# Seven products over 1024 tokens, in six accumulator banks, with every engine in written order

## The chip, the cores and the metric

The kernel runs on one NeuronCore of one Trainium2 chip. The metric is the device time of one execution in microseconds (us). Smaller is better. A core has a matrix engine (PE, TensorE), a vector engine (DVE), an activation engine (ACT), a general engine (POOL, GpSimd), and queues from which DMA transfers are issued; SP, the sync engine, issues nearly all of them here.

## The reference

`x` is 2048 tokens of 576 numbers, all in fp32. Everything starts from the layer norm `xn` of `x`.

- Branch A is a sliding-window attention: `xn @ wqkv`, 32 heads of 18 numbers, each query sees itself and the 255 keys before it, then `@ wo`. Its result is `s`.
- Branch B is a gated unit that mixes along the tokens:

```python
z  = gelu(xn @ w_in)                 # 2048 x 4608
z1 = z[:, :2304]
z2 = layernorm(z[:, 2304:])          # over the 2304 columns
g  = w_sp @ z2 + b_sp[:, None]       # 2048 x 2048 times 2048 x 2304
B  = (z1 * g) @ w_out                # 2048 x 576
out = x + s * silu(B)
```

The product `w_sp @ z2` is the largest piece of arithmetic in the kernel. "The spatial stage" below is this product, the bias, and the multiplication with `gelu(z1)`.

## The kernel before

**fp32 on the matrix engine.** A number is split into a high part that the engine can hold and the rest: `split(hi, lo, src)` (L105 to L107) copies `src` to `hi` on ACT, and subtracts `hi` from `src` into `lo` on DVE. A product of two split operands takes three passes: high by high, high by low, low by high. So each operand of a matmul costs one ACT and one DVE instruction first, and the DVE one waits for the ACT one.

**The stages, in order of time.** (1) Layer norm of `x`, transposition, split, and the products for q and k. (2) The values, then the second half of `w_in` with its gelu (`z2`, stored to `z2_d` in DRAM, L588 to L605), while POOL forms four sums and differences of the quarters of `w_sp` (`sp_combos`, `S1` to `S4`, stored to `sc_d`). (3) Attention in 16 units of four heads and half of the tokens each; the first half of `w_in` (`z1`, before its gelu, stored to `z1_d`) is threaded into it as filler. For each unit the row maxima of the next one are found early (`row_max`), and `RM0`, `RM1`, `RMN` say over which share of the unit they are spread. (4) The output projection of the attention, `wo_tile`, with the first forming of z blocks beside it. (5) The spatial stage. (6) The last stage: `y` from DRAM, split, times `w_out`, silu, and the end result.

**Seven products.** The spatial matrix and z2 are each cut in two by two blocks over the tokens, and the block product is done with seven block products instead of eight (the Strassen-Winograd form). Its left operands are `A11`, `A12`, `A22` of `w_sp` and the four stored combinations. Its right operands are seven z blocks, `zt[0]` to `zt[6]`: three normalized blocks of z2, and four sums or differences. `z_part` forms them block by block: `norm` loads 128 x 384 of z2 and normalizes it on DVE (`tensor_scalar`, L136); POOL forms the sums (L153 to L163).

**The loop of the spatial stage.** Columns of z2 are taken in `NG` = 3 groups of 384 column pairs. For each group there are two passes `c` over the output tokens, each 512 tokens of an output block. In each pass the seven products of `ORDER` run one after the other. `product` (L779 to L797) takes four steps `q`. A step loads 128 x 1024 of the left operand (`spr`), splits it into `sph` and `spl`, splits two z blocks at once (128 x 768 into `zh`, `zl`), and issues 18 matmuls of 512 columns into three accumulators (L794). Accumulators have two sides of three banks each, `acc00` to `acc02` and `acc10` to `acc12`. A finished product is evicted by `finish`, one product later, at `q` = 0 of the next: copies on ACT, sums on DVE and POOL, the gelu of `z1` on ACT (L814), the product with it on POOL (L815), and a store to `y_d`, which is issued one product later again. `work(3)` advances the forming of the z blocks of the next group (or the loading and splitting of `w_out` in the last group) by three small pieces per step.

**What sets the order.** From stage 2 to the end of stage 4 the PE, POOL and DVE instructions run in the order in which the program writes them (`manual_schedule`). In the spatial stage before the change no engine has a written order: a planner with a model of the times orders every engine's instructions. An engine works strictly in its order; an instruction that waits holds up what stands behind it on that engine. SP is such a queue for the DMAs.

Of the kernel before, what the change touches and what calls it, by code (L numbers as in the profile page):

```python
# [16 lines left out]
P = 128  # L17
S = 2048
D = 576
# [18 lines left out]
ZRB = 5  # L38
WCB = 3
RM0 = 0.0  # L40
RM1 = 0.78
# [14 lines left out]
def kernel(  # L56
# [22 lines left out]
    sc_d = dram.tile([4, 2, 4, P, 1024], F32, name="sc_d")  # L79
# [42 lines left out]
    def z_tile(from_pool, k):  # L122
        t = from_pool.tile([P, 2 * S if k < 4 else 8 * ZW], F32, name=f"b{k}")
        return t[:, :8 * ZW].rearrange("p (s c) -> p s c", s=8)

    def z_part(from_pool, g, k):


        def norm(i, j, s, dst=None):
            raw = from_pool.tile([P, ZW], F32, name="zr", bufs=ZRB)  # L130
            t = 8 * i + s
            c0 = j * FB + g * ZW
            sp.dma_start(raw, z2_d[t * P:(t + 1) * P, c0:c0 + ZW])
            yield
            dst = raw if dst is None else dst
            dve.tensor_scalar(dst, raw, mv2[:, t, 0:1], rstd2[:, t:t + 1], ALU.subtract, ALU.mult)  # L136
            yield dst

        def run(*gens):
            for n in gens:  # L140
                next(n)
            yield
            yield [next(n) for n in gens]

        for s in range(8):
            z = zt[k][:, s]
            if k in (0, 2, 6):
                yield from run(norm(int(k > 0), int(k == 6), s, z))
            elif k == 1:
                r = run(norm(1, 1, s), norm(0, 1, s))  # L150
                yield next(r)
                b22, b12 = next(r)
                pool.tensor_tensor(b22, b22, b12, ALU.subtract)  # L153
                pool.tensor_tensor(z, b22, zt[0][:, s], ALU.add)
                yield
            elif k == 4:
                r = run(norm(0, 1, s))
                yield next(r)
                b12, = next(r)
                pool.tensor_tensor(z, b12, zt[0][:, s], ALU.subtract)  # L160
                yield
            else:
                pool.tensor_tensor(z, *((zt[1][:, s], zt[0][:, s]) if k == 3 else (zt[2][:, s], zt[1][:, s])),  # L163
                                   ALU.subtract)
                yield

    xb = [xp.tile([P, 2 * S], F32R, name=f"b{k}").rearrange("p (a s) -> p a s", a=2) for k in range(4)]
    xt = xp.tile([P, S], F32R, name="tail")
    with ExitStack() as early:
        mmp = open_pool(early, "mmp", bufs=2, space=PSUM)  # L170
        zw = open_pool(early, "zw", bufs=2)
        def passes(wh, wl, xs):
            for k in range(4):
                yield wh[:, k], xb[k][:, 0, xs]
                yield wh[:, k], xb[k][:, 1, xs]
                yield wl[:, k], xb[k][:, 0, xs]
            yield wh[:, 4], xt[:, xs]
            yield wl[:, 4], xt[:, xs]
# [6 lines left out]
        with ExitStack() as ph:  # L185
# [23 lines left out]
            def norm_chunk(c):  # L209
# [19 lines left out]
                for k in range(5):  # L229
                    t = tp.tile([P, 512], F32, name="tpt")  # L230
                    for i in range(4):
                        pe.transpose(t[:, i * P:(i + 1) * P], xs[4 * c + i][:, k * P:(k + 1) * P], ident)
                    if k < 4:
                        split(xb[k][:, 0, cs], xb[k][:, 1, cs], t)
                    else:
                        act.activation(xt[:, cs], t, AF.Copy)
                        dve.tensor_tensor(xt[64:128, cs], t[64:128], f32(xt[64:128, cs]), ALU.subtract)
# [39 lines left out]
        with ExitStack() as ph:  # L277
# [234 lines left out]
            def sp_combos(stack):  # L512

                wc = open_pool(stack, "wc", bufs=WCB)
                steps = [(c, q, slice(h * 512, h * 512 + 512)) for c in range(2) for q in range(4) for h in range(2)]

                def load(c, q, cs):
                    ts = []
                    for n, (i, j) in (("a11", (0, 0)), ("a12", (0, 1)), ("a21", (1, 0)), ("a22", (1, 1))):
                        t = wc.tile([P, 512], F32, name=n)  # L520
                        sp.dma_start(t, w_sp[2 * i + c, 4 * j + q, :, cs])
# [4 lines left out]
                for n, (c, q, cs) in enumerate(steps):  # L526
# [10 lines left out]
                    for k, t in enumerate((a22, a11, a21, a12)):  # L537
                        sp.dma_start(sc_d[k, c, q, :, cs], t)
# [3 lines left out]
            with ExitStack() as gate:  # L542
# [26 lines left out]
                for pc in range(6):  # L569
# [13 lines left out]
                    for s in range(NS):  # L583
# [11 lines left out]
                        if s % 2 == 0:  # L595
                            zt = gz.tile([P, 2 * ZW], F32, name="zt")
                        zv = zt[:, s % 2 * ZW:s % 2 * ZW + ZW]
                        act.activation(zv, ps[:, :ZW], AF.Gelu_apprx_tanh)  # L598
                        dve.bn_stats(st2[:, s, pc, :], zv)  # L599
                        if s % 2 == 1:  # L600
                            act.dma_start(z2_d[(s - 1) * P:(s + 1) * P, zc].rearrange("(a p) c -> p a c", p=P),
                                          zt[:, :2 * ZW].rearrange("p (a c) -> p a c", a=2))
# [12 lines left out]
            raws = []  # L615
# [20 lines left out]
            with ExitStack() as heads:  # L636
# [7 lines left out]
                for u in range(NU):  # L644
# [11 lines left out]
                    for t, (s, j) in enumerate(items):  # L656
# [26 lines left out]
                        if u == NU - 1 and t == 30:  # L683
                            raws += [wo_load(0)]
# [10 lines left out]

        with ExitStack() as ph:
# [3 lines left out]
            def wo_tile(t):  # L700
                orw = raws[t]
# [5 lines left out]
                for c in range(2):  # L707
# [13 lines left out]
                    act.dma_start(s_d[rows, :], so)  # L721

            bb = xp.tile([P, S], F32, name="tail")
            zt = [z_tile(xp, k) for k in range(4)]

            def first_group():
                for k in range(4):
                    yield from z_part(zp, 0, k)

            head = first_group()  # L730
            raws += [wo_load(t) for t in range(1, 4)]
            for t in range(NS // 2):
# [3 lines left out]
                for _ in range(4):  # L736
                    next(head, None)
                if 1 <= t <= 4:
                    raws += [wo_load(t + 3)]
            for _ in head:  # L740
                pass
# [266 lines left out]
```

## Time and profile before

| | us |
|---|---|
| median of 3 runs (2181.55 to 2192.11) | 2190.79 |
| the profiled execution, whole | 2182.15 |
| its span, first to last instruction | 2180.4 |
| spatial stage, first to last of its 3024 matmuls | 1138.3 to 1932.4 |
| attention projection (stage 4), its matmuls | 1059.1 to 1128.6 |
| last stage, its matmuls | 1942.2 to 2175.3 |

The page of the profile gives busy times per engine, then groups of instructions by line with busy time, mean duration and the idle time just before them. Durations of matmuls overlap, because they are pipelined: the distance between two starts is what counts. A row of a window table gives the busy time (and the number of instructions) of PE, the weight load of PE, DVE, ACT and POOL, then the granted clock of PE as a share of full speed, the share of the DMA engines and GB/s. A row of the list of waits reads: who waited, for whom, us in total, how often, the longest.

### The profile page before, as it was taken

What the parts mean: (1) busy time and instruction counts of PE and PEld (TensorE: products, weight loads), DVE (VectorE), ACT (ScalarE), POOL (GpSimd) and SP (SyncE); (2) the same over time, 40 slices, a digit from 0 to 9 for tenths busy, and PEclk for the clock granted to TensorE, in tenths of its full rate; (3) what the DMA queues carried; (4) which work ended last, traced back from release to release, by engine and by line L of the source; (5) the groups of instructions that cost most, each with busy time, mean ns of one, the idle gap of its engine ahead of it and who ended that gap; (6) DMA issues with size and microseconds to landing.
All of it is one profiled execution on the core that took longest, in us unless ns stands there. A gap on an engine that the chain in (4) does not pass through costs nothing. (4 is left out here: it accounts for less than half of the span.)

```text
span 2180.4 us, 30948 instructions
## 1 busy us (share of the span) xinstructions
PE 2018.9 (93%) x11096; PEld 1661.3 (76%) x11096; DVE 1185.5 (54%) x2140; ACT 884.2 (41%) x1547; POOL 709.7 (33%) x624
## 2 busy tenths in 40 slices
PE   6999989989999999998879988899988999979999
PEld 5889989976666666665778766677676877769999
DVE  6411322465545555653277678766788667753331
ACT  3212212235545555555334453454434555532220
POOL 4001662012222222222083447734477343310000
PEclk9999999999999999999889999999999999999999
DMA  8655895234444545453585565655656555655441
GB/s 255 163 143 178 311 376 212 80 100 124 124 132 128 142 128 146 129 128 102 186 267 191 173 222 176 217 170 168 219 177 201 173 176 184 198 193 169 153 130 45
DMA packets 218986, 375.60 MB, mean 172 GB/s; under 512 B 43216, under 2 KB 115792, under 8 KB 218704
## 3 DMA queue, kind: packets, MB, share of 16 engines
q1 hardware_dynamic: 188688, 325.79, 49.3%
q10 hardware_dynamic: 30144, 47.83, 6.1%
q8 instruction: 87, 1.43, 0.3%
q14 instruction: 67, 0.55, 0.1%
HBM read 260.45 MB, written 112.83 MB: 171 GB/s over the span
## 5 line engine op out<-in xcount | busy, mean ns | idle before, releaser
L794 PE MATMUL acc<-spl,zh 128*128 128x512 f32 x1008 | 410.6, 407 | 48.4 <-DVE spl L107 48.1
L794 PE MATMUL acc<-sph,zl 128*128 128x512 f32 x1008 | 403.1, 400 | 0.0
L340 DVE CUSTOM_DVE_ANT_0 junk<-sp,band 128x384 bf16<-128x384 f32 (+1 forms) x512 | 267.6, 537 | 224.0 <-PE sp L336 219.4
L794 PE MATMUL acc<-sph,zh 128*128 128x512 f32 x1008 | 345.3, 397 | 25.4 <-ACT sph L106 25.4
L455 ACT ACTIVATE pt<-tps 128x384 f32<-128x384 f32 (+2 forms) x576 | 248.6, 438 | 230.7 <-PE tps L451 213.2
L107 DVE TENSOR_TENSOR zl<-b,zh 128x768 fp32r<-128x768 f32 x168 | 216.3, 1288 | 153.4 <-ACT zh L106 147.2
L794 PEld LDWEIGHTS acc<-spl,zh 128*128 128x128 f32 x1008 | 195.0, 193 | 117.1 <-DVE spl L107 77.1
L107 DVE TENSOR_TENSOR spl<-spr,sph 128x1024 fp32r<-128x1024 f32 x168 | 272.1, 1620 | 16.8 <-ACT sph L106 11.7
L106 ACT ACTIVATE zh<-b 128x768 fp32r<-128x768 f32 x168 | 141.4, 842 | 263.3 <-PE acc L794 251.7
L794 PEld LDWEIGHTS acc<-sph,zh 128*128 128x128 f32 x1008 | 192.0, 192 | 71.1 <-ACT sph L106 30.8
L384 PE MATMUL mm<-b,z1wh 128*128 128x512 f32 x576 | 231.6, 413 | 0.0
L794 PEld LDWEIGHTS acc<-sph,zl 128*128 128x128 f32 x1008 | 195.2, 194 | 39.6
L451 PE MATMUL tps<-att 128*128 128x384 f32 (+1 forms) x576 | 191.8, 333 | 32.7 <-ACT pt L455 19.5
L934 PE MATMUL po<-b,yh 128*128 128x288 f32 x1152 | 202.0, 298 | 9.4 <-ACT yh L106 9.4
L458 POOL TENSOR_SCALAR_AFFINE_SELECT pt<-pt 128x512 f32<-128x512 f32 x128 | 85.6, 669 | 380.3 <-ACT pt L455 370.7
L934 PEld LDWEIGHTS po<-b,yh 128*128 128x128 f32 x1152 | 171.2, 191 | 9.9 <-ACT yh L106 9.9
L336 PE MATMUL sp<-att 128*128 128x384 f32 (+1 forms) x512 | 176.5, 346 | 2.0 <-DVE mx L340 1.6
L106 ACT ACTIVATE sph<-spr 128x1024 fp32r<-128x1024 f32 x168 | 175.4, 1045 | 0.0
L588 PE MATMUL mm<-z2wh,b 128*128 128x384 f32 x640 | 166.1, 336 | 8.6 <-ACT zt L598 8.5
L451 PEld LDWEIGHTS tps<-att 128*128 128x128 f32 x576 | 110.0, 191 | 66.3 <-ACT pt L455 35.8
L599 DVE BATCH_NORM_STATS2 st<-zt 128x6 f32<-128x384 f32 x96 | 52.8, 558 | 180.2 <-ACT zt L598 180.2
L815 POOL TENSOR_TENSOR z1t<-z1t,cb 128x512 f32<-128x512 f32 x54 | 95.2, 1788 | 149.3 <-DVE cb L823 144.2
(154 smaller groups left out, 3214.8 us busy)
## 6 DMA issues: line engine op xcount, KB each, us to landing
spr<-sc_d SPq DMA_DIRECT2D x96, 512.0 KB
spr<-in_w_sp_dram SPq DMA_DIRECT2D x72, 512.0 KB
zr<-z_d SPq DMA_DIRECT2D x144, 192.0 KB
st_d<-qkhl SPq DMA_DIRECT2D x72, 256.0 KB
z_d<-zt ACTq DMA_DIRECT2D x48, 384.0 KB
z_d<-z1o ACTq DMA_DIRECT2D x72, 256.0 KB
z1t<-z_d SPq DMA_DIRECT2D x72, 256.0 KB
y_d<-z1t SPq DMA_DIRECT2D x72, 256.0 KB
```

The lines of the kernel that those rows point to most:

```text
L106: act.activation(hi, src, AF.Copy)
L107: dve.tensor_tensor(lo, src, f32(hi), ALU.subtract)
L336: pe.matmul(ps[:, :w], q_of(u, j)[:, i * P:(i + 1) * P], k_of(u, j)[:, k0:k0 + w], start=True, stop=True)
L340: dve.tensor_tensor_reduce(out=junk[:, :w], in0=ps[:, :w], in1=band[:, m0:m0 + w], scale=1.0, scalar=-3.0e38, op0=ALU.add, op1=ALU.max, ac ...
L384: pe.matmul(ps, w, r, start=n == 0, stop=n == len(pl) - 1)
L451: pe.matmul(ps[:, :m * P], k_of(u, j)[:, (kb - base) * P:(kb - base + 1) * P], q_of(u, j)[:, (a - lo) * P:(a - lo + m) * P], start=True, s ...
L455: act.activation(pt[:, j, d0:d0 + n * P], ps[:, (qa - a) * P:(qa - a + n) * P], AF.Exp, scale=scale)
L458: pool.affine_select(out=pt[:, :, 0:P], in_=pt[:, :, 0:P], pattern=[[0, 4], [1, P]], compare_op=ALU.is_ge, fill=0.0, base=0, channel_multi ...
L588: pe.matmul(ps[:, :ZW], r, wt, start=n == 0, stop=n == len(pl) - 1)
L794: pe.matmul(acc[p], z[:, s, ps], w[:, s], start=b and n == 0, stop=e and n == 2, skip_group_check=True)
L815: pool.tensor_tensor(zs[p], zs[p], blocks[p], ALU.mult)
L934: pe.matmul(po[i][:, a, :288], y[:, i * P:(i + 1) * P], w[:, a * 288:(a + 1) * 288], start=f == 0 and m == 0, stop=f == NF - 1 and m == 2)
```

## The change

- **Shape of a product.** The two passes `c` are merged: a product now covers 1024 output tokens. It has eight steps `s`, each with one z block of 128 x 384 and one 128 x 1024 tile of the left operand, and again 18 matmuls of 512 columns, now three into each of six accumulators. The six rotate through all eight banks. There are 168 steps as before; a z block is now split once per group, not twice. The layout of `w_sp` in DRAM, `sc_d` and the loop of `sp_combos` follow.
- **Order of the products.** `A11` times z block 0, then `A12` times 2 added on top, then `S2`·1, `S3`·3 on top, `S1`·4, `S4`·6 on top, and `A22`·5. An accumulator opens anew at products 0, 2, 4 and 6 (`OPENS`).
- **No POOL work in the stage.** Normalizing goes from DVE to ACT (`Identity` with the reciprocal deviation as scale and `nmr2` as bias); sums of z blocks, sums of accumulators and the products with gelu go from POOL to DVE.
- **Written order.** All five engines run the spatial stage in program order. In the iteration of step m the program writes: the matmuls of step m; if it ends a product, its eviction; the load of the left operand for step m+4; both splits for step m+2; one or two z units (`pump`: the forming of a unit is written two units behind its loads); four deferred pieces (`run_lazy`: loads and gelus of `z1`, bias sums, products, stores).
- **The start.** The load and the splits of step 0 are written into stage 4, in a pool of their own (`w0p`), and five z blocks are formed there (four before). `b_sp` is loaded at the beginning of stage 4.
- **The end.** In the last group 14 of the 18 tiles of `w_out` are loaded and split beside the products; the other four in the last stage, one after the other through one buffer. `y` is split into eight buffers of three row tiles; its chunks are taken in the order 0 to 7.
- **Elsewhere.** `xb` and `xt` become six tiles of equal size with the same contents (`plane`), the weights of `z1` and `z2` go to the other side of the on-chip memory, the z2 result has four buffers (two before), `WCB` goes from 3 to 2, `RM1` from 0.78 to 0.70, the buffers of `zr` from 5 to 6.

The core of the diff, with the new loop:

```diff
-ORDER = [(A11, "a"), (S2, "b"), (A12, "a"), (S3, "b"), (S1, "c"), (A22, "d"), (S4, "c")]
+PRODUCTS = [(A11, 0), (A12, 2), (S2, 1), (S3, 3), (S1, 4), (S4, 6), (A22, 5)]
...
+    def split_step(m):
+        if m < len(order_sp):
+            g, n, s = order_sp[m]
+            h = [w_tile(m, [P, w], F32R, t) for t, w in
+                 (("sph", 1024), ("spl", 1024), ("zh", ZW), ("zl", ZW))]
+            split(h[2], h[3], zt[PRODUCTS[n][1]][:, s])
+            split(h[0], h[1], raws.pop(m))
+            halves[m] = h
...
+        ph.enter_context(tc.manual_schedule(engines={
+            mybir.EngineType.PE, mybir.EngineType.Activation, mybir.EngineType.DVE, mybir.EngineType.Pool,
+            mybir.EngineType.SP}))
...
+        def evict(g, n):
+            if n == 0:
+                st["t1"] = tiles("t1")
+                for j in range(6):
+                    act.activation(st["t1"][j], acc[j], AF.Copy)
+                st["z"] = z1_load(g, 0, 0)
+            elif n == 1:
+                gate(g, 0, 0, st["z"], plus(acc, lambda j: bias(j, 0)))
+            elif n == 2:
+                st["u2"] = tiles("u2")
+                for j in range(6):
+                    dve.tensor_tensor(st["u2"][j], acc[j], st["t1"][j], ALU.add)
+                    lazy.append(lambda j=j, u=st["u2"]: dve.tensor_tensor(u[j], u[j], bias(j, 0), ALU.add))
...
+        for m, (g, n, s) in enumerate(order_sp):
+            k = PRODUCTS[n][1]
+            if s == 0 and n in OPENS:
+                acc = [accp.tile([P, 512], F32, name=f"acc{(base + j) % 8}") for j in range(6)]
+                base += 6
+            wh, wl, zh, zl = halves.pop(m)
+            for j in range(6):
+                c, p = divmod(j, 3)
+                cs, ps = slice(c * 512, c * 512 + 512), slice(p * P, p * P + P)
+                for i, (z, w) in enumerate(((zh, wh), (zh, wl), (zl, wh))):
+                    pe.matmul(acc[j], z[:, ps], w[:, cs], start=s == i == 0 and n in OPENS,
+                              stop=s == 7 and i == 2, skip_group_check=True)
+            if s == 7:
+                evict(g, n)
+            load_w(m + 4)
+            split_step(m + 2)
+            pump(2 if len(units) > 4 else 1)
+            run_lazy(4)
```

`w_tile(m, ...)` takes its buffer from `w0p` for every third step and from a pool of two for the others, so three steps can be held. `gate` puts six products and six stores into the deferred list, `z1_load` six loads and six gelus.

392 lines of the change are left out of this document (182 added, 210 removed).

## The prediction

> **What bounds the kernel now.** I read the page first, then a table of windows cut at the stages, then who made PE wait.
>
> ```profile
> PE 2018.9 (93%) x11096; PEld 1661.3 (76%) x11096; DVE 1185.5 (54%) x2140; ACT 884.2 (41%) x1547; POOL 709.7 (33%) x624
> ```
>
> ```profile
> core 0: us, PE busy (x) PEld busy (x) DVE busy (x) ACT busy (x) POOL busy (x), PEclk, DMA share, GB/s
> 247.20:458.00 210.80, 202.25 (x1154) 198.77 (x1153) 78.10 (x172) 44.93 (x92) 74.66 (x56) 1.00 0.60 217
> ...
> 1138.30:1932.40 794.10, 729.99 (x3023) 576.21 (x3024) 592.81 (x532) 376.59 (x476) 380.74 (x227) 0.97 0.59 189
> 1460.00:1500.00 40.00, 39.77 (x175) 32.26 (x174) 28.70 (x26) 20.40 (x26) 14.71 (x9) 1.00 0.53 169
> 1932.40:1942.20 9.80, 0.40 (x2) 0.00 (x0) 1.20 (x2) 0.84 (x1) 3.69 (x3) 0.75 0.63 192
> 1942.20:2175.30 233.10, 233.00 (x1728) 232.76 (x1728) 67.41 (x108) 49.29 (x79) 0.00 (x0) 0.99 0.44 137
> ```
>
> PE is the bound, and the question is how far each stage is from PE's own pace. In the spatial stage a good stretch (1460 to 1500) issues 175 matmuls in 40.00 us, 0.2286 us each. At that pace its 3024 matmuls take 691 us; they take 794.1. So **103 us** of the stage are not matmul work, and no change that keeps 3024 matmuls of this form can gain more there. The last stage runs without gaps.
>
> ```profile
> PE acc L794 <- DVE spl L107: 48.1, 50, 3.8
> PE acc L794 <- ACT sph L106: 25.4, 12, 9.8
> ```
>
> PE waits for the splits: 73.5 us, of which 9.8 lie before the first matmul of the stage. Of the 103, then, some 64 are these waits; the granted clock of 0.97 costs 0.03 x 794 = 24; the rest, 15, is small gaps. The clock is a consequence of the waits:
>
> ```profile
> 1574.51 0.50 PE L794 MATMUL acc<-spl,zh 128*128 128x512 f32 x1 [2.46 <-DVE spl L107]
> ...
> 1575.65 0.63 PE L794 MATMUL acc<-spl,zh 128*128 128x512 f32 x1
> 1576.08 0.63 PE L794 MATMUL acc<-sph,zl 128*128 128x512 f32 x1
> ...
> 1578.64 0.49 PE L794 MATMUL acc<-sph,zl 128*128 128x512 f32 x1
> ```
>
> After a wait of 2.46 us, matmuls start 0.43 us apart instead of 0.23, from 1575.65 to 1578.64: seven of them, and with the two at the edges some 1.6 us lost. [...] So waits of two to four us are priced with 1.6 us on top.
>
> Why is the split late?
>
> ```profile
> 1914.60 1.23 DVE L107 TENSOR_TENSOR spl<-spr,sph 128x1024 fp32r<-128x1024 f32 x1 [0.63 <-DMA wr<-in_w_out_dram]
> ...
> 1918.54 2.31 DVE L107 TENSOR_TENSOR spl<-spr,sph 128x1024 fp32r<-128x1024 f32 x1
> 1920.77 2.05 DVE L107 TENSOR_TENSOR zl<-b,zh 128x768 fp32r<-128x768 f32 x1
> 1922.74 1.21 DVE L107 TENSOR_TENSOR spl<-spr,sph 128x1024 fp32r<-128x1024 f32 x1
> ```
>
> ```profile
> 1916.51 5.50 POOL L815 TENSOR_TENSOR z1t<-z1t,cb 128x512 f32<-128x512 f32 x3 [10.21 <-DVE cb L823]
> ```
>
> The same subtraction takes 1.23 us alone and 2.31 while POOL multiplies. POOL is busy for 381 of the 794 us, so up to half of the splits can be of the slow kind, and they queue behind loads in an order that a planner chose.
>
> **The change, part by part.** The prices come from these groups:
>
> ```profile
> L107 DVE TENSOR_TENSOR yl<-yr,yh 128x768 fp32r<-128x768 f32 x48 | 44.5, 956 | 68.6 <-ACT yh L106 68.5
> L949 DVE TENSOR_TENSOR fx<-fx,fs 128x288 f32<-128x288 f32 x32 | 13.1, 452 | 0.0
> L823 DVE TENSOR_TENSOR cb<-acc,t 128x512 f32<-128x512 f32 x36 | 22.7, 681 | 2.7 <-PE acc L794 2.7
> L106 ACT ACTIVATE sph<-spr 128x1024 fp32r<-128x1024 f32 x168 | 175.4, 1045 | 0.0
> L106 ACT ACTIVATE zh<-b 128x768 fp32r<-128x768 f32 x168 | 141.4, 842 | 263.3 <-PE acc L794 251.7
> L814 ACT ACTIVATE z1t<-z1t 128x512 f32<-128x512 f32 x72 | 45.3, 630 | 129.1 <-DMA z1t<-z_d 106.0 <-issue 22.6
> L110 ACT ACTIVATE sd<-mv,eps_t 128x4 f32<-128x4 f32 x3 | 0.9, 297 | 5.6 <-DVE mv L222 5.6
> ```
>
> *DVE.* A subtraction of 384 columns: between 452 (288 wide) and 956 (768 wide, no POOL work in that stage), by a line 553 ns. A step needs 1.22 + 0.55 = 1.77 us. Per group of 56 steps: 56 x 1.77 = 99.3; z sums 16 + 8 + 8 + 8 = 40 x 0.553 = 22.1; accumulator sums, bias sums and products 36 + 12 + 24 = 72 x 0.681 = 49.0. Together 170 us. PE needs 56 x 18 x 0.2286 = 230 us. So DVE is 74% full although it takes over POOL's work, because the splits fall back to their undisturbed length and the z split halves. *ACT.* A copy of 384: on the line through 842 and 1045, 0.54 us. Normalizing on ACT is in no row; it lies between that 0.54 and, with two operands per partition, 0.78 (297 ns for four columns against about 236 on the line puts one such operand at 0.06, and I allow twice that for each). I take 0.66. Per group 56 x 1.585 + 48 x 0.66 + 6 x 0.6 + 24 x 0.63 = 139 us, 60%. Neither is the bound on average. *DMA*: the same bytes (189 GB/s x 794 us) in 700 us, 214 GB/s, below the 217 that stage 2 had.
>
> *Cover.* The splits of step m+2 can start when step m-1 has freed its buffers and must be done at the end of m+1: two steps, 2 x 4.11 = 8.23 us, for 1.77 of DVE. This lead is what hides everything, so I walk its worst place, the end of the third product, where DVE evicts and also forms block 1. After PE's last matmul: last eviction done at 0.8; splits 1.77; two z units of two sums 2.21; four bias sums 2.72; the next splits 1.77. Sum 9.27 against 8.23: **1.0 us late**. With z blocks of one sum (ends of products 3, 4, 6, counted from 0) the sum is 8.17, just on time; elsewhere shorter. The banks cost nothing: bank j is complete three matmuls x (6 - j) before the end of a product and is wanted again in the same order. So 3 x 1.0, and I add 4 for the ends without margin. Stage: 691 + 7 + 5 (below, first steps and hand-overs) = **703, so -91 us**. Ends: -103, and -36 (the first rival).
>
> *The start of the stage.*
>
> ```profile
> 1081.22 47.34 PE L716 MATMUL wops<-att,ohl 128*128 128x288 f32 x332 [4.34 <-DVE ohl L705]
> 1138.32 1.65 PE L794 MATMUL acc<-sph,zh 128*128 128x512 f32 x3 [9.76 <-ACT sph L106]
> ```
>
> PE stands 9.8 us. After the change step 0 is split in stage 4, and PE waits only for the last eviction there, about 1.5. Step 1's operand lies in memory that stage 4 frees; load, ACT and first matmul take some 6 us against 1.5 + 4.1, so 1 to 2 us more. **-8**, between 0 and -9.
>
> *Stage 4 itself* now forms five z blocks instead of part of four, and `b_sp` (1 MB, 5 us at 217 GB/s) is loaded ahead of the rows that `wo_tile` wants. DVE has 32 sums x 0.55 = 18 us there without POOL's disturbance. **+2**, -5 to +8.
>
> *Stage 2.*
>
> ```profile
> PE mm L588 <- ACT zt L598: 8.7, 9, 2.9
> ACT zt L598 <- DMA z_d<-zt: 21.0, 6, 4.3
> ```
>
> Four buffers take away the wait of ACT for stores; PE can gain at most its 8.7. `WCB` = 2 makes SP wait for each store of a combination before the next load, 16 times, ahead of weights that have a step of slack. **-5**, -9 to +8.
>
> *`RM1`*: the maxima end earlier in a unit, so their way through DRAM ends earlier; PE's waits for it:
>
> ```profile
> PE tps L451 <- DMA att<-m_d: 13.0, 6, 6.2
> ```
>
> The 6.2 is the first unit's, which `RM1` does not touch; 6.8 is the most to gain, and denser maxima load DVE more. **-1**, -6 to +6.
>
> *The end of the stage.*
>
> ```profile
> 1932.38 3.71 POOL L815 TENSOR_TENSOR z1t<-z1t,cb 128x512 f32<-128x512 f32 x3 [10.37 <-DVE cb L823]
> ...
> 1936.49 1.54 SPq L911 DMA_DIRECT2D yr<-y_d  x3
> ...
> 1941.34 0.84 ACT L106 ACTIVATE yh<-yr 128x768 fp32r<-128x768 f32 x1 [13.75 <-issue]
> ```
>
> PE stands 9.8 us: POOL's three products, stores, then 4.85 for the load of `y`. After: last eviction 0.8, six products on DVE 4.1, perhaps a split of `w_out`, stores, the same load, 0.85: about 12. **+2**, -2 to +6. In the last stage four tiles of `w_out` come one by one, a load of up to 4.85 and a split of 1.4 each, from some 14 us after the last product: ready at 20, 26, 32 and 38. PE takes 12 x 233.1 / 1728 = 1.62 us per row tile in the first chunk, so it wants the first of them at 12 + 14 x 1.62 = 35, the last at 40. **+1**, 0 to +8. `plane`, sides of the memory and chunk order: nothing, the same instructions on the same data.
>
> Sum: -91 - 8 + 2 - 5 - 1 + 2 + 1 = **-100 us**, from the profiled execution's 2182.15 to 2082. The median of the runs stands 8.6 above the profiled execution, with one run of three at its level; I add 3: **2085 us**.
>
> **Rivals.**
>
> *DVE is the next bound (chance 0.15).* For it: 74% on average and no margin at four ends of products per group. If DVE's work took 30% longer (waits between its instructions, ACT and DVE handing over halves), the third product's end is late by 1.0 + 0.3 x 9.27 = 3.8, the three marginal ones by 2.4 each, two others by 1 or 2: 14 per group, 42 in all, plus 12 slow starts x 1.6 = 19. Stage 752, total about 2134. Against it: undisturbed DVE durations scatter by hundredths (1.21, 1.23), and the stage without POOL work runs them at 956.
>
> *The written order holds the loads up (0.06), slower than before.* SP has one queue: a store of a product waits at its head for DVE, and the load for step m+4 stands behind it. A load is written 4 steps = 16.5 us before PE wants it; minus 4.85 landing and 2.3 splitting, 9.3 us of slack. If SP is held about 13 us at each of the 21 ends, PE stands 3.7 and loses 1.6 to the clock: 21 x 5.3 = 111 on top of 703, total 2196, slower. It decides from a hold of 12.3 us (a loss of 100 / 21 = 4.8). Against it: the store is written six pieces, one and a half steps, behind its product. [...]
>
> *The change does not do what it says (0.06).* Of the waits only the part that POOL's disturbance made goes, and ACT, now ordered, stands behind gelus that wait for `z1` (106 us of ACT's waits are for that load): half of the 91 stays, 2130 to 2150; or all of it, within 0.5% (0.02).
>
> *Better (0.07)*: the walk's lateness does not show, stage 2 gains its 8.7 and the start its 9: 2050 to 2062.
>
> **How the numbers follow.** Forecast (2062 to 2110): 0.64. About 0.5% is what can be told from no change here. Faster: 0.64 + 0.15 + 0.06 + 0.07 = 0.92; same 0.02; slower 0.06. The range reaches down into the better case and up to the end of the DVE rival, 2055 to 2136; outside are the upper part of "does not do", "same", "slower" and a little below.
>
> **What would show it.** POOL at 0 in the stage; `spl` at 1.22 and a z split near 0.55 in every instance; 3024 matmuls in about 700 us at a clock of 0.99 or more; PE's waits for `spl` and `sph` under 10 us, the longest in the second and third step after the third product; one wait near 2 us at the start. DVE near 510 us busy in the stage, ACT near 420. Wrong if PE still waits tens of us for splits, if SP's rows show issues held for over 10 us, or if the stages before 1056 move by more than 10 us.

## The result and the profile after

The changed kernel takes **2075.29 us** (median of 4 runs, 2071.18 to 2077.59); the kernel before took 2188.66 in the same comparison (four runs, 2181.55 to 2192.11; the table above has three of them). The ratio is **0.9484**, 95% interval 0.9454 to 0.9514: faster. The forecast was 2085 us, with a range of 2055 to 2136.

Windows of the changed kernel, cut at the same events as those of before (columns as there): stage 2, attention, stage 4 up to the first spatial matmul, the spatial stage, and then the page's line of all engines.

```profile
205.20:446.80 241.60, 238.85 (x1376) 237.69 (x1376) 90.38 (x190) 58.74 (x116) 88.17 (x66) 1.00 0.68 240
446.80:1056.70 609.90, 565.85 (x3491) 384.82 (x3490) 311.59 (x1096) 317.27 (x742) 154.56 (x242) 0.98 0.49 128
1056.70:1136.90 80.20, 67.89 (x449) 66.45 (x450) 32.51 (x52) 43.74 (x64) 0.00 (x0) 0.89 0.67 220
1136.90:1828.70 691.80, 688.02 (x3026) 568.33 (x3024) 466.94 (x643) 368.16 (x544) 0.00 (x0) 1.00 0.65 215
```

```profile
PE 1981.8 (95%) x11096; PEld 1653.4 (80%) x11096; DVE 1054.3 (51%) x2260; ACT 898.8 (43%) x1655; POOL 280.9 (14%) x360
```

The spatial stage went from 794.3 us to 691.8, on PE's own pace, with POOL at 0 and a granted clock of 1.00. The same cuts on the trace of before:

```profile
208.10:457.90 249.80, 241.06 (x1376) 237.32 (x1376) 90.38 (x190) 55.47 (x112) 88.52 (x66) 1.00 0.65 231
457.90:1059.10 601.20, 560.18 (x3492) 386.10 (x3490) 312.53 (x1096) 319.62 (x742) 157.99 (x242) 0.98 0.48 129
1059.10:1138.30 79.20, 64.66 (x448) 63.86 (x448) 45.22 (x56) 22.96 (x29) 40.58 (x36) 0.89 0.72 232
1138.30:1932.60 794.30, 730.18 (x3024) 576.21 (x3024) 593.01 (x532) 376.59 (x476) 380.94 (x227) 0.97 0.59 189
```

Window by window: stage 2 -8.2, attention +8.7, stage 4 with the hand-over +1.0, spatial stage -102.5. The span of the profiled execution went from 2180.4 to 2075.8 us, -104.6; what is left of that is -2.9 before stage 2, +0.4 between the spatial and the last stage, -1 in the last stage. So the gain is the spatial stage; the rest nearly cancels, though not as forecast.

The groups and the list of PE's waits show why:

```profile
L107 DVE TENSOR_TENSOR spl<-spr,sph 128x1024 fp32r<-128x1024 f32 x168 | 205.2, 1221 | 39.8 <-ACT sph L106 34.7 <-DMA s_d<-so 4.4 <-DMA z1t<-z_d 0.8
L107 DVE TENSOR_TENSOR zl<-b,zh 128x384 fp32r<-128x384 f32 x168 | 93.0, 554 | 168.1 <-ACT zh L106 168.0
L144 ACT ACTIVATE b<-zr,nmr,rstd 128x384 f32<-128x384 f32 x72 | 48.4, 696 | 8.4 <-DMA zr<-z_d 8.4
```

```profile
PE acc L906 <- DVE spl L107: 3.5, 1, 3.5
```

The two subtractions of a step take their undisturbed 1221 and 554 ns on average. Of the 73.5 us for which PE waited for splits, one wait of 3.5 is left. It is step 1 of the stage: DVE's `spl` stood 4.4 us until the store of stage 4's last output tile had landed (`DMA s_d<-so`); the buffer of `spl` seems to lie where that tile was.

### The profile page after: what moved, and what is told of

It reads as the page before. It is cut to its first block, busy times and chain, and to the rows that moved or that the text cites. A ratio compares the mean times of both kernels' runs of the same rounds, so it can differ in the third digit from the quotient of the medians.

```text
span 2075.8 us, 30675 instructions
## 1 busy us (share of the span) xinstructions
PE 1981.8 (95%) x11096; PEld 1653.4 (80%) x11096; DVE 1054.3 (51%) x2260; ACT 898.8 (43%) x1655; POOL 280.9 (14%) x360
## 4 chain that ended last, share of the span: by engine, by line
PE 80%; DMA 11%; DVE 3%; issue 2%; ACT 2%; SPq 1%; POOL 0%; ACTq 0%; DVEq 0%; POOLq 0%
PE acc L906 31%; PE po L963 11%; PE mm L625 8%; PE mm L421 8%; PE mm L285 5%; PE tps L488 4%; PE ops L511 4%; DMA att<-st_d 4%; PE sp L373 3%; PE vps L439 3%; DMA zr<-z_d 2%; DMA z1raw<-in_w_z_dram 2%; PE wops L755 1%; DMA rp<-r_d 1%; DVE junk L377 0%
## 5 line engine op out<-in xcount | busy, mean ns | idle before, releaser
L906 PE MATMUL acc<-sph,zh 128*128 128x512 f32 x1008 | 392.9, 390 | 0.0
L421 PE MATMUL mm<-b,z1wh 128*128 128x512 f32 x648 | 255.7, 407 | 0.0
L488 PE MATMUL tps<-att 128*128 128x384 f32 (+1 forms) x576 | 197.7, 343 | 37.1 <-ACT pt L492 27.8
L107 DVE TENSOR_TENSOR spl<-spr,sph 128x1024 fp32r<-128x1024 f32 x168 | 205.2, 1221 | 39.8 <-ACT sph L106 34.7
L106 ACT ACTIVATE zh<-b 128x384 fp32r<-128x384 f32 x168 | 87.7, 522 | 265.5 <-PE acc L906 265.1
L625 PE MATMUL mm<-z2wh,b 128*128 128x384 f32 x720 | 192.1, 335 | 2.7 <-ACT zt L635 2.7
L107 DVE TENSOR_TENSOR zl<-b,zh 128x384 fp32r<-128x384 f32 x168 | 93.0, 554 | 168.1 <-ACT zh L106 168.0
L963 PE MATMUL po<-b,yh 128*128 128x288 f32 x896 | 156.5, 297 | 9.8 <-ACT yh L106 9.8
L421 PEld LDWEIGHTS mm<-b,z1wh 128*128 128x128 f32 x648 | 122.2, 191 | 35.3 <-issue 21.5
L421 PE MATMUL mm<-b,z1wl 128*128 128x512 f32 x360 | 146.0, 406 | 0.0
L963 PEld LDWEIGHTS po<-b,yh 128*128 128x128 f32 x896 | 132.8, 190 | 10.3 <-ACT yh L106 10.3
```

The costliest lines, as they stand in the source:

```text
L106: act.activation(hi, src, AF.Copy)
L107: dve.tensor_tensor(lo, src, f32(hi), ALU.subtract)
L421: pe.matmul(ps, w, r, start=n == 0, stop=n == len(pl) - 1)
L488: pe.matmul(ps[:, :m * P], k_of(u, j)[:, (kb - base) * P:(kb - base + 1) * P], q_of(u, j)[:, (a - lo) * P:(a - lo + m) * P], start=True, s ...
L625: pe.matmul(ps[:, :ZW], r, wt, start=n == 0, stop=n == len(pl) - 1)
L906: pe.matmul(acc[j], z[:, ps], w[:, cs], start=s == i == 0 and n in OPENS, stop=s == 7 and i == 2, skip_group_check=True)
```

## The experiments

### Order, lead and GpSimd, each alone

Four kernels take one property each. `a2_planner` drops the written order:

```diff
-        ph.enter_context(tc.manual_schedule(engines={...}))
```

> The changed kernel without the written order in the spatial stage: the same instructions, but the planner orders all engines there. Its stage took 691.6 us with the written order, 794.1 before the change. Theory A (the lead of two steps that the written order guarantees is needed, beside the absence of GpSimd work): the planner puts z sums, products and loads in front of some splits, PE waits at the ends of products, stage 710 to 740 us, whole 2095 to 2125. Rival B (GpSimd's disturbance of VectorE was all, and the order does not matter): stage at most 697 us, whole within 6 us of 2075.

`a3_one_ahead` keeps the order and shortens the lead, of the splits from two steps to one and of the loads from four to three (the new z tiles are opened one step later, since the last split of a block is now written later):

```diff
-            load_w(m + 4)
-            split_step(m + 2)
+            load_w(m + 3)
+            split_step(m + 1)
...
-            if s == 5:
+            if s == 6:
```

> The changed kernel with the splits written one step ahead instead of two, and the loads three instead of four. Theory A: at the end of each product the eviction now stands on VectorE in front of the split for the very next step: 0.8 for the last bank, 0.55 and 1.22 for the split, less one matmul, so PE waits some 2.3 us, and 1.6 more go to the slow clock, at 20 ends: stage 740 to 770 us, whole 2125 to 2155. Rival B (no lead is needed once GpSimd is idle, because VectorE is only 74% full): stage at most 700 us, whole at most 2085.

`a4_pool` gives POOL the products and bias sums (of `u2` and of `t1`) back, with order and lead kept (the bias sum of `t1` is edited like that of `u2`):

```diff
-                return lambda: dve.tensor_tensor(zs[n], zs[n], blocks[n], ALU.mult)
+                return lambda: pool.tensor_tensor(zs[n], zs[n], blocks[n], ALU.mult)
...
-  lazy.append(lambda j=j, u=st["u2"]: dve.tensor_tensor(u[j], u[j], bias(j, 0), ALU.add))
+  lazy.append(lambda j=j, u=st["u2"]: pool.tensor_tensor(u[j], u[j], bias(j, 0), ALU.add))
```

> The changed kernel with the products with gelu(z1) and the bias sums on GpSimd again (36 instructions of 512 columns per group), in the same written order. Rival C (order and lead are all, GpSimd's work does no harm): stage within 3 us of 691.6, or shorter, since VectorE has 25 us less to do per group. Theory A: while GpSimd works, VectorE's splits take up to 2.3 us instead of 1.22; four pieces of GpSimd work behind each product's end lengthen four splits by about 1.1 each, 4.4, against 2.7 us that VectorE is spared: 1.7 us later at most ends, stage 697 to 715 us, whole 2080 to 2098. The subtraction of 1024 columns should have a mean above 1.4 us.

`b1_no_pool` starts from the kernel before and only moves the POOL work of the spatial stage away, all of its sums like the product shown:

```diff
-            dve.tensor_scalar(dst, raw, mv2[:, t, 0:1], rstd2[:, t:t + 1], ALU.subtract, ALU.mult)
+            act.activation(dst, raw, AF.Identity, scale=rstd2[:, t:t + 1], bias=nmr2[:, t:t + 1])
...
-                pool.tensor_tensor(zs[p], zs[p], blocks[p], ALU.mult)
+                dve.tensor_tensor(zs[p], zs[p], blocks[p], ALU.mult)
```

> The kernel before with one part of the change alone: in the spatial stage GpSimd's sums and products go to VectorE and the normalizing to ScalarE; passes of 512 tokens, planner and everything else stay. Rival B (GpSimd's disturbance was all): stage at most 705 us instead of 794, whole at most 2100. Theory A (disturbance and missing lead each have a part): the subtractions fall to 1.22 and 0.96 us, but PE still waits for splits behind other work, stage 730 to 760 us, whole 2125 to 2155. Rival C (order alone): 785 to 800 us, whole within 10 us of 2189.

| kernel | spatial stage, us | whole, us | ratio to before (95%) |
|---|---|---|---|
| a2_planner | 701.2 | 2082.01 | 0.9572 (0.9540 to 0.9605) |
| a3_one_ahead | 763.0 | 2150.03 | 0.9885 (0.9843 to 0.9927) |
| a4_pool | 703.2 | 2084.83 | 0.9579 (0.9535 to 0.9623) |
| b1_no_pool | 765.5 | 2146.88 | 0.9879 (0.9834 to 0.9925) |

(The kernel before had a median of 2178.31 beside these runs.) The window of the spatial stage of `a3_one_ahead`, and its wait:

```profile
1130.50:1893.50 763.00, 713.96 (x3026) 580.42 (x3024) 467.15 (x643) 367.73 (x544) 0.00 (x0) 0.97 0.59 195
```

```profile
PE acc L905 <- DVE spl L107: 42.9, 22, 3.5
```

Same work on DVE (467 us), no POOL, same order: only the lead is shorter, and PE waits 22 times for `spl`, about once per end of a product, 2.0 us each. That is the expected mechanism and size (740 to 770). The **lead** is worth 71 us here. The **written order** is worth some 10 us: the planner comes to 701.2, below the 710 that theory A set, above rival B's 697; neither is quite right, and the order was overrated. **POOL** costs 11 us even with full lead, and that with 158 us of its work in the stage instead of 381: `a4_pool` lands in its range, with the subtraction of 1024 columns at a mean of 1389 ns, just below the 1400 expected. And taking POOL's work out of the kernel before (`b1_no_pool`) gave only 29 of the 102; the 765.5 is a little worse than the 730 to 760 expected. Its waits:

```profile
PE acc L798 <- ACT sph L106: 34.5, 18, 11.0
PE acc L798 <- DVE spl L107: 22.5, 33, 1.5
```

### The lead in the kernel before

If the lead is the larger part, it should help the kernel before too. It has two buffers for the halves of a step, so the split for step q+2 can start only when step q is done. `b2_three` gives it three; `b3_three_nopool` has that and the edit of `b1_no_pool` (`spl`, `zh` and `zl` are edited like `sph`; to make room, both have one buffer less for `spr`, as shown, for `zr` and for the raw tiles of `w_out`):

```diff
-                raw = wsp.tile([P, 1024], F32, name="spr", bufs=3)
+                raw = wsp.tile([P, 1024], F32, name="spr", bufs=2)
...
-                wh = wsp.tile([P, 2, 512], F32R, name="sph", bufs=2)
+                wh = wsp.tile([P, 2, 512], F32R, name="sph", bufs=3)
```

> The kernel before with three buffers instead of two for the split halves (sph, spl, zh, zl), so that splits can stand two steps ahead; two buffers instead of three for the raw tiles, four instead of five for zr and one instead of two for w_out make the room. GpSimd works as before, the planner orders. Theory D (the lead of one step was the larger part of the loss before, since taking it away from the changed kernel cost 71 us): stage 794 to 725 - 750 us, whole 2110 to 2140. Rival B (GpSimd's disturbance is the larger part): stage 780 to 800.

> Both parts in the kernel before: three buffers for the split halves, and GpSimd's work of the spatial stage on VectorE and ScalarE; passes of 512 tokens in three banks and the planner stay. Theory D (lead and undisturbed VectorE together are the whole gain; six banks, the merged passes, the halved z split and the written order add little): stage 697 to 715 us, whole 2080 to 2100. Rival E (VectorE, with the z blocks split twice per group, 580 us of work, and three banks evicted one product later do not keep up): stage 730 to 765.

| spatial stage, us | two buffers | three buffers |
|---|---|---|
| POOL works | 794.3 (before) | 779.7 (b2) |
| POOL idle | 765.5 (b1) | 712.1 (b3) |

```profile
1140.50:1852.60 712.10, 697.27 (x3024) 566.67 (x3024) 531.12 (x647) 439.97 (x582) 0.00 (x0) 1.00 0.65 209
```

```profile
1133.40:1913.10 779.70, 723.79 (x3024) 579.44 (x3024) 592.04 (x530) 375.91 (x474) 387.02 (x228) 0.97 0.60 192
```

Theory D fails for `b2_three`: three buffers alone give 15 us, at the edge of rival B's range, not 44 to 69. With POOL idle as well they give 53 more than `b1_no_pool`. Alone the two parts are worth 15 and 29, together **82**. Each stage time is one trace, but the whole times, of four or five runs each, say the same: 18, 31 and 81 us below the kernel before beside them. The subtraction of 1024 columns in `b2_three`, then in `b3_three_nopool`:

```profile
L107 DVE TENSOR_TENSOR spl<-spr,sph 128x1024 fp32r<-128x1024 f32 x168 | 274.2, 1633 | 37.5 <-ACT sph L106 36.9
L107 DVE TENSOR_TENSOR spl<-spr,sph 128x1024 fp32r<-128x1024 f32 x168 | 205.0, 1221 | 30.6 <-ACT sph L106 29.3
```

With POOL working, the third buffer is there but the splits are still slow, 1633 ns on average: of the 37 waits of PE for over 0.4 us in that stage, 30 have a subtraction of over 1.3 us in the 8 us before them. In `b3_three_nopool` no subtraction is slow and 14 such waits are left. This fits splits that have no time to get ahead; it is not shown that it is the whole reason. The share of time that DVE is busy is not the reason: it is 76% in `b2_three` and 75% in `b3_three_nopool`, where DVE has taken over POOL's work and given the normalizing to ACT (647 instructions for 530) and is still busy for 61 us less. The last 20 us, from 712.1 to 691.8, belong to the written order, the six banks, the merged passes, the halved z split and the loads further ahead, together; 10 of them went when the written order was dropped from the changed kernel. Whole times: b2 2164.76, ratio 0.9918 (0.9890 to 0.9945), above theory D's range; b3 2102.60, ratio 0.9639 (0.9608 to 0.9670), with its stage as expected and its whole 2.6 us above the range.

### How full VectorE may be

`a6_zsplit_twice` repeats the z split of each step; `a8_dvepad` adds as much DVE time with an instruction that nobody waits for (and undoes the two edits of stage 2, for the next question):

```diff
# a6_zsplit_twice
             split(h[2], h[3], zt[PRODUCTS[n][1]][:, s])
+            split(h[2], h[3], zt[PRODUCTS[n][1]][:, s])
# a8_dvepad
             split(h[0], h[1], raws.pop(m))
+            if m > 1:
+                pad = st2.rearrange("p a b c -> p (a b c)")[:, :ZW]
+                dve.tensor_tensor(pad, band[:, :ZW], band[:, :ZW], ALU.add)
...
-WCB = 2
+WCB = 3
-                            zz = gz.tile([P, 2 * ZW], F32, name="zt", bufs=4)
+                            zz = gz.tile([P, 2 * ZW], F32, name="zt", bufs=2)
```

> The changed kernel with the split of the z block done twice in every step, the work the kernel before had: VectorE gets 0.55 us more per step, 201 of 230 us per group, 87%. Theory A: the walk at the third product's end lengthens from 9.27 to 10.4 us against 8.23; measured lateness was 0.4 where the walk said 1.0, so 1.5 late there and about 0.4 at three other ends, stage 695 to 705 us, whole 2078 to 2090. Rival F (VectorE is nearly the bound already, each end then runs late and cools the clock): stage above 720.

> The changed kernel with one more addition of 384 columns on VectorE per step of the spatial stage, from a constant into memory that nobody reads, so that nothing waits for it; it adds 0.55 us per step, as splitting z twice did, but no hand-over between ScalarE and VectorE. And, for stage 2, the two edits of the change there undone together: two buffers for the z2 result and WCB = 3. Theory A' (the z split done twice took 85 us because ScalarE and VectorE then hand each step's halves to and fro, not because VectorE was full): spatial stage 694 to 705 us. Rival F (VectorE at 87% is the bound): above 740. Stage 2: if WCB gave its gain, 248 to 252 us from first to last matmul instead of 241.6; if neither edit did, within 3 us of 241.6.

The spatial stage of each (`a6_zsplit_twice` first), and the wait of ACT that belongs to `a6_zsplit_twice`:

```profile
1131.70:1908.10 776.40, 723.53 (x3026) 572.38 (x3024) 559.34 (x810) 438.31 (x711) 0.00 (x0) 0.98 0.59 191
```

```profile
1145.70:1842.70 697.00, 690.46 (x3026) 567.67 (x3024) 539.45 (x809) 367.96 (x544) 0.00 (x0) 1.00 0.65 213
```

```profile
ACT zh L106 <- DVE zl L107: 315.7, 167, 5.0
```

`a6_zsplit_twice` took 776.4 us (whole 2159.95, ratio 0.9905, 0.9870 to 0.9939) where 695 to 705 were expected; rival F's "above 720" came true, but not by its cause. The experiment asked two things at once: the second copy to `zh` must wait until DVE has read the first one, so ACT waits for DVE in 167 of 168 steps, and `sph` of the same step stands behind it. `a8_dvepad`, run once (whole 2092.46), adds the same DVE time without the hand-over, and the stage takes 697.0 us, as theory A' said: 540 us of DVE in 697 are no bound. What the wrong guess showed is worth as much: 85 us from one wait per step of ACT for DVE and the second copies, which keep ACT busy for 70 us more; the two were not taken apart.

### Stage 2

`a7_zt2` undoes only the four buffers (`bufs=4` to `bufs=2` for the z2 result):

```diff
-                            zz = gz.tile([P, 2 * ZW], F32, name="zt", bufs=4)
+                            zz = gz.tile([P, 2 * ZW], F32, name="zt", bufs=2)
```

> The changed kernel with two buffers for the z2 result instead of four. If the buffers gave the 8.3 us that stage 2 gained (249.9 to 241.6 us from its first to its last matmul), stage 2 goes back to 247 to 251; if something else did, it stays within 2 us of 241.6.

Stage 2 of `a7_zt2` (run once, whole 2072.72), then of `a8_dvepad` (two buffers and `WCB` = 3):

```profile
206.40:450.00 243.60, 239.80 (x1378) 237.68 (x1376) 89.03 (x190) 55.94 (x112) 89.64 (x66) 1.00 0.68 237
```

```profile
206.80:458.10 251.30, 242.84 (x1378) 238.97 (x1376) 89.11 (x190) 55.55 (x112) 88.22 (x66) 0.99 0.65 230
```

With two buffers for the z2 result the stage takes 243.6 us at `WCB` = 2 and 251.3 at 3: most of the 8 us come from **fewer** buffers for the combinations of `w_sp`. What `WCB` = 3 costs beside four buffers was not run. A window around the place where PE stood, in the kernel before and after:

```profile
265.00:295.00 30.00, 23.63 (x132) 22.35 (x131) 6.14 (x11) 6.35 (x13) 20.11 (x16) 1.00 1.02 364
```

```profile
265.00:295.00 30.00, 27.25 (x155) 26.44 (x154) 7.41 (x13) 7.07 (x14) 17.22 (x13) 1.00 1.00 353
```

The DMA engines are saturated there in both (shares of 1.02 and 1.00, 364 and 353 GB/s). That fewer buffers keep the loads of the combinations from crowding the stores of z2 fits, since POOL does fewer combinations in that window (13 instructions for 16) and PE more matmuls; this reason was not tested, and each reading is one trace.

### Attention and `RM1`

`a1_rm78` sets the old value in the changed kernel:

```diff
-RM1 = 0.70
+RM1 = 0.78
```

> The changed kernel with RM1 = 0.78 as before. From the end of stage 2 to the first matmul of stage 4, six runs with 0.70 took 603.5 to 610.9 us, four with 0.78 592.8 to 601.1. Theory G (the denser row maxima cost it): back to 593 to 601 us, whole 5 to 12 us below 2075. Rival (the order that the planner finds for ScalarE and SP with the other memory layout costs it): 603 to 611, whole unchanged.

```profile
445.40:1043.20 597.80, 556.28 (x3491) 384.69 (x3489) 312.33 (x1095) 319.07 (x742) 156.04 (x242) 0.98 0.48 130
```

Attention took 597.8 us, inside theory G's 593 to 601, and the whole 2067.21 (2062.80 to 2069.03, ratio 0.9477, 0.9454 to 0.9500). But the ratio's interval covers that of the changed kernel, and a second kernel with 0.78 (`c2_late_pump`, below) had 603.4 us. Over all traces: with 0.70 603.5 to 610.9 (eight, mean 606.0); the changed kernel with 0.78 597.8 and 603.4; the kernels built on the one before, with 0.78, 592.8 to 601.1 (four). So 0.70 did not help, and probably cost about 5 us; the rest of the +8.7 stays open.

PE's waits tell the two sides of it. The changed kernel, then `a1_rm78`; `m_d` are the row maxima on their way through DRAM, `pt` the exponentials that ACT makes of PE's scores:

```profile
PE tps L488 <- ACT pt L492: 27.8, 22, 4.9
PE tps L488 <- DMA att<-m_d: 6.1, 1, 6.1
```

```profile
PE tps L488 <- ACT pt L492: 16.9, 11, 5.3
PE tps L488 <- DMA att<-m_d: 13.4, 6, 6.0
```

With 0.70 PE waits 5.8 to 6.1 us for maxima in all eight traces, with 0.78 11.3 to 14.1 in all six. But it waits 24.2 to 29.3 us for ACT's exponentials, against 16.6 to 19.5: what was gained in one place was lost in the other.

### Stage 4

`a5_stage4_dve` normalizes the z blocks of stage 4 on DVE instead of ACT; `c2_late_pump` (with `RM1 = 0.78`) leaves them on ACT and starts later:

```diff
# a5_stage4_dve, in form()
-                act.activation(dst, raw, AF.Identity, scale=..., bias=...)
+                if len(wpools) < 2:
+                    dve.tensor_scalar(dst, raw, mv2[:, t, 0:1], rstd2[:, t:t + 1], ALU.subtract, ALU.mult)
+                else:
+                    act.activation(dst, raw, AF.Identity, scale=..., bias=...)
# c2_late_pump, in wo_tile()
-                    pump(3)
+                    pump(4 if t >= 2 else 0)
```

> The changed kernel with the normalizing of the z blocks in stage 4 on VectorE (one tensor_scalar each) instead of ScalarE; the spatial stage keeps it on ScalarE. Theory H (stage 4 lost its 10.5 us because evictions of the projection stand on ScalarE behind normalizations that wait for their rows): from the first matmul of stage 4 to the first of the spatial stage 69 to 74 us instead of 80.2, whole 6 to 11 us less. Rival I (the rows of z2 arrive too slowly, on whichever engine they are waited for): 78 us or more, whole unchanged.

> The changed kernel with RM1 = 0.78, and with the z units of stage 4 left out behind the first two tiles of the projection and written four instead of three behind each half tile after that. Moving the normalizing to VectorE left stage 4 at 79.1 us, with PE waiting 12.4 us for VectorE's splits in place of ScalarE's evictions, so the wait for rows is what moves along. Theory J (the rows are late only early in the stage, where they compete with the projection's own loads and the last division's way through DRAM; from the fourth tile on DMA is half idle, 0.53): from the first matmul of stage 4 to the first of the spatial stage 70 to 75 us instead of 79.2, whole 2057 to 2063 against 2067 for RM1 = 0.78 alone. Rival K (the rows are needed in this stage anyway and the waits only move to later tiles or to the start of the spatial stage): 78 us or more, or the first steps of the spatial stage longer by as much; whole 2064 to 2070.

PE's waits in stage 4: the changed kernel, then `a5_stage4_dve`; then the window of `c2_late_pump`.

```profile
PE wops L755 <- ACT so L758: 8.6, 3, 4.0
PE wops L755 <- DVE ohl L744: 3.6, 1, 3.6
```

```profile
PE wops L758 <- DVE ohl L747: 12.4, 3, 6.1
...
PE wops L758 <- ACT so L761: 0.5, 1, 0.5
```

```profile
1049.70:1123.90 74.20, 64.75 (x448) 62.78 (x449) 32.91 (x52) 43.24 (x64) 0.00 (x0) 0.95 0.74 237
```

`a5_stage4_dve` left the stage at 79.1 us (whole 2071.52, ratio 0.9492, 0.9469 to 0.9516), not at theory H's 69 to 74. PE's 12 us of waiting changed engines and kept its length. Rival I's number came true, but rows of z2 are only a part of the cause. In front of PE's longest wait in the changed kernel, 4.0 us, ACT stood for a row and then normalized five blocks; in front of the longest in `a5_stage4_dve`, DVE stood for the operand of the last division of the attention, and the split of the next tile stood behind that division:

```profile
1075.47 1.30 ACT L144 ACTIVATE zr<-zr,nmr,rstd 128x384 f32<-128x384 f32 x2 [5.91 <-DMA zr<-z_d]
```

```profile
1072.44 1.23 DVE L540 TENSOR_TENSOR oul<-oul,att 128x1024 f32<-128x1024 f32 x1 [6.88 <-DMA att<-r_d]
1073.59 1.22 DVE L747 TENSOR_TENSOR ohl<-att,ohl 128x1024 fp32r<-128x1024 f32 x1
```

```profile
1074.86 8.84 PE L758 MATMUL wops<-att,ohl 128*128 128x288 f32 x52 [6.12 <-DVE ohl L747]
```

The other long wait of `a5_stage4_dve`, 5.9 us, came behind normalizations and sums that the edit had put on DVE; its waits for rows add up to 7.9 us, in ten pieces. The late row of the changed kernel was the first that SP issued behind the load of that operand (1065.67 and 1065.00). So work that needs a transfer stands in front of what PE needs, on either engine; which transfer is to blame stays open.

Forming the blocks later took the stage to 74.2 us, in theory J's range and 5 us below the 79.2 of `a1_rm78`, which differs in this edit alone; the first spatial steps did not grow (690.2 us, there 690.0). The whole came to 2064.84 (2064.30 to 2070.33), ratio 0.9486 (0.9464 to 0.9508): above theory J's 2057 to 2063, in rival K's range. Attention, which the edit does not touch, took 5.6 us longer in this trace than in that of `a1_rm78`. So the stage is 5 us shorter, but no version is shown to be faster as a whole than the changed kernel: the kernel before was 2179.25 beside this run and 2188.66 beside the changed one.

## Why the prediction was right, and where not

The whole came out closer than its parts: -104.6 between the profiled executions, forecast -100. The spatial stage and stage 2 gave more than forecast, stage 4 and the attention cost more, and both of these lay outside the ranges given for them. That the errors nearly cancel is luck. The 3 us added for the median were not needed either: the median lies 2.3 us below the profiled execution's 2077.59.

**Spatial stage: -102.5, forecast -91 (703 us against 691.8).** The mechanism held: POOL at 0, splits at their undisturbed length, the waits for splits gone, the clock at 1.00. Two terms were too large. *Pace:* the "good stretch" of 0.2286 us still held small gaps; from 1500 to 1820 the changed kernel starts 1412 matmuls, 0.2267 us apart, which makes 685 us for 3024. *The ends of products, 7 us:* the walk found the right place, and only there was anything lost. DVE's rows behind the third product's end, then PE's:

```profile
1241.07 0.55 DVE L107 TENSOR_TENSOR zl<-b,zh 128x384 fp32r<-128x384 f32 x1
...
1247.68 1.22 DVE L107 TENSOR_TENSOR spl<-spr,sph 128x1024 fp32r<-128x1024 f32 x1
```

```profile
1248.42 0.39 PE L906 MATMUL acc<-sph,zh 128*128 128x512 f32 x1
1248.95 0.50 PE L906 MATMUL acc<-spl,zh 128*128 128x512 f32 x1
```

The second matmul of step 26 starts 0.53 instead of 0.23 after the first, because the split ends at 1248.90; with a slower one behind it, 0.4 us are lost, once in each of the first two groups. The forecast said 1.0 in each of three, and 4 more for other ends, where nothing was lost. In these rows a DVE instruction that does not read the result of the one ahead starts about 0.08 us before that one is over (1241.07 + 0.55 against the next start at 1241.54), so the twelve of them at such a place take less than the sum of their durations; the walk added durations. The 467 us for which DVE was busy, instead of 510, are largely the same error: the durations add up to 498. ACT was busy for 368 instead of about 420, and its durations add up to 401. *First steps, 5 us:* the size was right (one wait of 3.5 and seven slow matmuls), the mechanism only in part: the forecast was a wait of 1 to 2 us for the load and the copy on ACT, and it was the buffer of `spl` that came late.

**The start and stage 4: -6 forecast, +1.0 measured.** PE's 9.8 us before the stage did go, to 0.1. Stage 4 then took 80.1 us instead of 69.5 for the same 448 matmuls, outside the -5 to +8 given. The step that failed is "+2": it counted the load of `b_sp` and DVE's busy time, and put at nothing that evictions and splits of the projection now stand on their engines behind work that waits for transfers (5.91 us on ACT in the row of the changed kernel above). `a5_stage4_dve` shows that moving the work to DVE does not help, `c2_late_pump` that 5 us go when it comes later. The remark that `b_sp` is now loaded first was empty: the planner had already issued that load at the beginning of stage 4 before the change.

**Stage 2: -5 forecast, -8.2 measured, for the wrong reason.** Four buffers were priced as the gain and `WCB` = 2 as a loss; two buffers again cost 2 us, and `WCB` = 3 with them 9.7. That the total came near is luck.

**`RM1`: -1 forecast, +8.7 measured in that window,** outside -6 to +6. The waits for maxima on their way through DRAM had 6.8 us to give, and gave 6.9 (13.0 to 6.1). What failed is that nothing was put against it: PE's waits for ACT's exponentials grew from 19.5 to 27.8 us. Part of the loss is scatter.

**The end: +2 and +1 forecast; +0.4 and -1 measured.** The products on DVE took 3.8 us, the split of the first `y` started 3.5 us after its load was issued (4.85 before).

**The rivals.** "DVE is the next bound": `a8_dvepad` puts 15% more on it for 5 us. "Written order holds the loads up": in the stage no store of `y_d` waited more than 2.0 us at SP's head for its product, and ACT's `sph` waited 2.5 us in all for its loads; the order gave 10 us. (The hold from which this rival decides is 9.3 + 4.8 - 1.6 = 12.5 us, not 12.3.) "Only the part that POOL's disturbance made goes": this is `b1_no_pool`, 29 of 102, and it would have been the result without the lead. The forecast named both parts; it did not see that each gives less than a third without the other.

## To carry to other kernels

When an engine feeds PE step by step, ask how many steps ahead it may run (its buffers) and whether it has time to get there (its load, with disturbances): alone they gave 15 and 29 us of 102 here, both 82. One wait per step of ACT for DVE, with the copy that brought it, cost 85 us here; as much more work on DVE without such a wait, which left it 77% busy, cost 5. And where work that waits for a transfer stands in front of what PE needs, moving it to another engine moved the wait (PE's 12 us of waiting changed engines, and the stage took 79.1 us against 80.2); moving it to a later place shortened the stage from 79.2 us to 74.2.

## What the runs showed of the hardware

The price of a wait in clock is not fixed. The same wait at step 1, 3.3 to 3.6 us long, was followed by seven matmuls at half pace in the changed kernel (0.43 us apart instead of 0.23) and eleven in `a5_stage4_dve`, but by none in `a1_rm78`, `a7_zt2` and `c2_late_pump`. The granted clock in that stretch of the changed kernel (1145.5 to 1148.6) was 0.50; from 1137 to 1141 and from 1149 to 1153 it was 1.00. In `a3_one_ahead` 17 of PE's 25 waits for splits were 2.16 us long. Ten of them were followed by seven or eight slow matmuls, seven by none. One of each kind:

```profile
1279.71 0.50 PE L905 MATMUL acc<-spl,zh 128*128 128x512 f32 x1 [2.16 <-DVE spl L107]
...
1280.75 0.63 PE L905 MATMUL acc<-spl,zh 128*128 128x512 f32 x1
1281.17 0.63 PE L905 MATMUL acc<-sph,zl 128*128 128x512 f32 x1
```

```profile
1243.84 0.50 PE L905 MATMUL acc<-spl,zh 128*128 128x512 f32 x1 [2.16 <-DVE spl L107]
...
1244.65 0.40 PE L905 MATMUL acc<-spl,zh 128*128 128x512 f32 x1
1244.88 0.40 PE L905 MATMUL acc<-sph,zl 128*128 128x512 f32 x1
```

The 25 waits were followed by 95 slow matmuls in all; each loses 0.2 us, so that is 0.76 us per wait. In `b1_no_pool` the 50 waits for splits inside the stage, 0.9 us long on average, were followed by 39, 0.16 us per wait. The 1.6 us of the forecast is what one such stretch of slow matmuls costs; it was charged to every wait. What decides whether slow matmuls follow a wait was not shown.

Normalizing on ACT with two operands per partition took 696 ns for 384 columns, against 660 in the forecast and 522 for a plain copy of that size.
